# Two attention sums and one sum of activations, each at another place in VectorE's queue, in an attention and MLP block

## The chip, the cores and the metric

The kernel runs on one core of one Trainium2 chip. The metric is the time of one execution on the device in microseconds (us), inputs and outputs in the chip's memory. Engines go by these names: PE is TensorE (matmuls; PEld its weight loads), DVE is VectorE, ACT is ScalarE, POOL is GpSimd, and SP issues the DMA transfers. Each engine works through its own queue of instructions strictly in order; an instruction that waits for another engine holds up all that stand behind it in its queue.

## The reference

One block, on 2048 tokens of width 576, in float32:

```
xn  = layernorm(x)
q, k, v = xn @ wqkv                      # 32 heads of 18
att = softmax over 8 keys (this token and 7 before it, every second one) of q.k / sqrt(18)
out = x + (att @ v) @ wo + mish(xn @ w1 + b1) @ w2      # w1: 576 x 4608, w2: 4608 x 576
```

Tokens before the first are masked out of the softmax. All inputs and outputs are float32.

## The kernel before, in words

**Precision.** A float32 matrix is held as a high part in a rounded matmul format and a low part, the rest. A product is then three matmuls: high by high, high by low, low by high. Each operand made on the chip therefore takes two steps: ACT casts the high part (`u_high`, L820), and DVE or POOL subtracts it from the original to get the low part (`u_low`, L826).

**Tiling.** The tokens are done in two halves of 1024, each in blocks of 512. The 4608 hidden units are taken 256 at a time; one such step is called q. For each q, `m1_part` computes the hidden units of a half in six parts (numbered 0 to 5) out of blocked sums, in the manner of Strassen and Winograd, into three PSUM tiles h1, h2 and h3 (tag `h`, 4 buffers). ACT and DVE bring them to SBUF tiles (ACT copy at L714, DVE addition at L725, ACT Mish at L726). These activation tiles have the names `ra`, `rm`, `rt` with a number, and `ra_r`.

**The seven-product stage.** In the second half, the steps q = 0 to 7 are joined in pairs, e = 0 to 3, and the product with w2 of a pair is done as seven items (e, k), k = 0 to 6, of the products named P7, P4, P1, P5, P2, P6, P3 in that order. Each item is one call of `p_item`: 24 matmuls (L872) into four PSUM tiles `po` (tag `out`, 4 buffers), whose left operands are two tiles `u` (`u_e_k_0` and `u_e_k_1`, qq = 0 and 1) and whose right operand `pw` is fetched from memory. Each `po` is then added to an accumulator `accP...` by DVE (L878), or in the first pair, for three of the products, copied by ACT (L876). With four buffers, the first `po` of an item cannot begin before the first `po` of the item before has been read. Some left operands are sums of activations (`u_sum`, L814, on DVE or POOL), made in place in an activation tile.

**Attention alongside.** Attention needs no PE. It runs on POOL, DVE and ACT behind the matmuls, as a generator that goes on by one step at chosen places. A step multiplies on POOL, in two instructions (L539 for q by k, tiles `pr`; L577 for weights by v, tiles `pv`; the two share two buffers), and a DVE reduction sums the product (L544 into `L`, or L583 into `og`): these reductions are the attention sums. The sum of one step is kept back in `behind` and issued by `flush()` when the next step begins.

**What sets the order.** `plan` is a list of slots. Each slot has one part of PE's work (an `m1_part`, an item, a chunk of a product), and a list of background functions that `before(slot, fn)` puts there. For each slot the program issues, in this order: things left over for the beginning (`first`), the background functions, then what mish left pending in the slot before (`held`), then the slot's own work; and at the very end what lies in `tail`. Since each engine keeps the order in which its instructions were issued, this list is the schedule. `flush()` (L515 on) has three ways: normally the attention sum is issued at once, ahead of the slot's own additions; if the slot is in `behind_adds`, the sum goes to `tail`, behind everything of the slot; if it is in `behind_next`, it goes to the background list of the next slot.

The places of `u_sum`, `u_high` and `u_low` of an item come from a table of three numbers per (k, qq), `ds`: slots relative to that of the item. Slots are named by `at[...]`: `at["p", "x", e, k]` is that of the item (e, k), and `at["s", 1, q, i]` the i-th slot of step q in the second half.

Of the kernel before, what the change touches and what calls it, by code (L numbers as in the profile page):

```python
# [31 lines left out]
OC = 4  # L32
# [7 lines left out]
def block_kernel(ctx: ExitStack, tc: tile.TileContext, x, wq, wo, w1, b1, w2, mask, out):  # L40
# [469 lines left out]
    behind_adds, behind_next, now = set(), set(), [0]  # L510
# [296 lines left out]
    def u_sum(e, k, qq):  # L807
        name, q = LEFT[ORD[k]], 2 * e + qq
        eng = nc.gpsimd if (name, qq) in (("S1", 1), ("S4", 0)) else nc.vector
        x, y, op = dict(S3=("A11", "A21", ALU.subtract), S2=("A22", "S3", ALU.subtract), S1=("A11", "S2", ALU.add),  # L810
                        S4=("A12", "S2", ALU.subtract)).get(name, (None,) * 3)
        if x:
            t = rslotof(q, SLOT[name])
            eng.tensor_tensor(out=t, in0=u_src(q, x), in1=u_src(q, y), op=op)  # L814
            held_[q, SLOT[name]] = name
# [21 lines left out]
    def p_fetch(e, k):  # L837
        name = RIGHT[ORD[k]]
        t = pw[e, k] = sb.tile([P, 2, 2, HC], F32R, tag="w2", bufs=4, name=f"pw_{e}_{k}")
        nc.sync.dma_start(t.bitcast(F32), kept[name, e])  # L840
# [315 lines left out]
    at = {}  # L1156
# [7 lines left out]
    def before(i, fn):  # L1164
        plan[max(i, 0)][1].append(fn)
# [190 lines left out]
    def spot(hf, q, i):  # L1356
        return at["s", hf, q, i]
# [67 lines left out]
    for g, (e, k, s) in enumerate(items):  # L1425
        lead = items[g - 3][2] if g >= 3 else spot(1, 0, 5) + 2 * g
        before(lead + 1, lambda e=e, k=k: p_fetch(e, k))
        for qq in range(2):
            ds = {(0, 0): (-6, -5, -5), (0, 1): (-2, -1, -1), (1, 0): (0, -4, -2), (1, 1): (0, -2, -2), (2, 0): (0, -3, -2), (2, 1): (0, -3, -2), (3, 0): (-4, -3, -2), (3, 1): (-4, -2, -1), (4, 0): (0, -3, -3), (4, 1): (0, -3, -2), (5, 0): (-1, -3, -3), (5, 1): (0, -3, -2), (6, 0): (-4, -3, -1), (6, 1): (-4, -3, -2)}[k, qq]
            if (e, k, qq) == (OC - 1, 0, 0):  # L1430
                ds = (-5, -4, -4)
            if e == 0 and k in (3, 5):
                ds = (-3, -2, -1) if k == 3 else (1,) + ds[1:]
            for d, f in zip(ds[1:], (u_high, u_low)):
                before(s + d, lambda f=f, e=e, k=k, qq=qq: f(e, k, qq))
            s2 = items[7 * e + (0 if k == 5 else k)][2] + ds[0]
            before(s2, lambda e=e, k=k, qq=qq: u_sum(e, k, qq))
# [22 lines left out]
    for n in range(8):  # L1460
        c, k = divmod(n, 4)
# [30 lines left out]


    att = {}
    behind_adds.add(at["p", "x", OC - 1, 4])
    behind_next.add(at["m", 1, 10, 3])
    T = [0.0]
    for p_ in plan:
# [17 lines left out]
    k = marks[0] - 1  # L1516
    for n in range(steps - len(last_steps)):
        t = 6.111 * n
        k = next(k for k in range(k + 1, len(plan)) if T[k + 1] > t and ok[k])
# [21 lines left out]
    for n, name in enumerate(("T3", "T1", "T2", "T4", "B11", "B21", "B22", "R", "D")):  # L1541
        k = i + 10 + (2, 5, 10, 15, 20, 25, 30, 35, 40)[n]
# [77 lines left out]
```

## Time and profile before

| | us |
|---|---|
| median of 3 runs | 1109.92 |
| lowest and highest of them | 1109.09, 1110.12 |
| the profiled execution, own time | 1110.25 |
| its span, first to last instruction | 1108.5 |
| PE busy | 1100.6 |
| DVE busy | 851.2 |
| POOL busy | 789.4 |
| ACT busy | 499.1 |

The granted TensorE clock is at full speed over the whole span. The seven-product stage runs in the trace from about 625 to 827 us. Of the views used below: the chain of waits is the work that ended last, followed back from the end, with start, length and engine of each piece; the timeline lists the instructions of an engine with start (us), length (us), engine, line, what is written from what, the shape, and, in square brackets, how long the engine sat idle before it and for whom. An instruction's length overlaps a little with the start of the next; where the pace counts, differences of starts are taken.

### The profile page before, as it was taken

The numbers are of one execution on the slowest core, as the hardware profiler recorded it, in microseconds if no ns is written. First come the engines' busy times: TensorE is split into PE (matmuls) and PEld (weight loads), VectorE is DVE, ScalarE is ACT, GpSimd is POOL, SyncE is SP. The second block draws the span as 40 slices with busy tenths as digits, with TensorE's granted clock in tenths as the row PEclk, the third lists the DMA queues.
The fourth block names the chain that finished last, engine by engine and source line by source line (L and its number), as shares of the span: only waits on it lengthen the run. The fifth ranks groups of instructions, "written<-read, shape, count | busy, mean of one in ns | idle before, by whom it ended". The sixth has DMA issues, their size and how long they took to land.

```text
span 1108.5 us, 18208 instructions
## 1 busy us (share of the span) xinstructions
PE 1100.6 (99%) x6550; PEld 1014.4 (92%) x6550; DVE 851.2 (77%) x1367; ACT 499.1 (45%) x917; POOL 789.4 (71%) x639
## 2 busy tenths in 40 slices
PE   8999999999999999999999999999999999999998
PEld 7999899999999999999999888989899999999998
DVE  6368788888889888898656577777876677777786
ACT  5444655544545543545333354434433344343353
POOL 2479777776779688685789666667598976867542
PEclk9999999999999999999999999999999999999999
DMA  5899696868777768675598799656664657776674
GB/s 197 285 310 309 234 341 237 282 235 264 256 262 247 263 227 295 235 265 216 169 323 269 237 360 315 224 190 208 222 223 171 210 195 222 241 290 216 182 232 141
DMA packets 178271, 271.60 MB, mean 245 GB/s; under 512 B 53219, under 2 KB 120069, under 8 KB 178181
## 3 DMA queue, kind: packets, MB, share of 16 engines
q1 hardware_dynamic: 178180, 270.44, 71.8%
q8 instruction: 52, 0.85, 0.3%
q14 instruction: 39, 0.31, 0.1%
HBM read 160.39 MB, written 110.00 MB: 244 GB/s over the span
## 4 chain that ended last, share of the span: by engine, by line
PE 94%; DMA 2%; DVE 1%; ACT 1%; POOL 1%; issue 1%; SPq 0%; DVEq 0%; POOLq 0%
PE h L680 29%; PE po L780 21%; PE po L893 11%; PE pq L348 11%; PE po L872 7%; PE h L686 6%; PE o L1076 5%; PE z L446 4%; DMA acc<-in_x 1%; DMA accP<-in_x 1%; POOL act L732 0%; PE ta L75 0%; DVE rm L814 0%; DVE og L583 0%; ACT u L820 0%
## 5 line engine op out<-in xcount | busy, mean ns | idle before, releaser
L780 PEld LDWEIGHTS po<-w,act 128*128 128x128 f32 x1728 | 236.4, 188 | 6.0 <-POOL act L732 0.4
L780 PE MATMUL po<-w,act 128*128 128x288 f32 x1728 | 240.7, 295 | 0.2 <-POOL act L732 0.2
L539 POOL TENSOR_TENSOR pr<-q,kv 128x576 f32<-128x576 f32 x128 | 197.3, 1568 | 9.6 <-DMA q<-q_d 6.5
L732 POOL TENSOR_TENSOR act<-c,act 128x512 fp32r<-128x512 f32 x81 | 107.2, 1324 | 128.4 <-ACT act L731 127.8
L577 POOL TENSOR_TENSOR pv<-L,kv 128x576 f32<-128x576 f32 x128 | 178.1, 1484 | 24.8 <-DVE L L570 19.9
L784 DVE TENSOR_TENSOR acc<-po,acc 128x288 f32<-128x288 f32 x288 | 119.6, 450 | 30.0 <-PE po L780 28.8
L348 PE MATMUL pq<-wq,xt 128*128 128x432 f32 x672 | 136.4, 361 | 1.5 <-ACT xt L81 1.4
L893 PEld LDWEIGHTS po<-w,act 128*128 128x128 f32 x960 | 130.9, 188 | 2.9
L893 PE MATMUL po<-w,act 128*128 128x288 f32 x960 | 132.9, 294 | 0.0
L348 PEld LDWEIGHTS pq<-wq,xt 128*128 128x128 f32 x672 | 125.0, 188 | 8.4 <-ACT xt L81 2.4
L726 ACT ACTIVATE c<-c,b1c 128x512 f32<-128x512 f32 x81 | 58.7, 725 | 137.8 <-DVE c L725 137.6
L680 PE MATMUL h<-S,t 128*128 128x512 f32 x432 | 110.5, 391 | 0.0
L680 PE MATMUL h<-xt,t 128*128 128x512 f32 x432 | 110.5, 391 | 0.0
L583 DVE TENSOR_REDUCE og<-pv 128x144 f32<-128x1152 f32 x64 | 85.9, 1345 | 24.0 <-POOL pv L577 23.9
L680 PE MATMUL h<-xt,wa 128*128 128x512 f32 x432 | 104.1, 390 | 0.0
L714 ACT COPY c<-h 128x512 f32<-128x512 f32 x81 | 47.4, 586 | 124.2 <-PE h L686 73.1
L544 DVE TENSOR_REDUCE L<-pr 128x64 f32<-128x1152 f32 x64 | 85.8, 1342 | 19.7 <-POOL pr L539 19.6
L680 PEld LDWEIGHTS h<-xt,wa 128*128 128x128 f32 x432 | 80.9, 188 | 17.0
L872 PEld LDWEIGHTS po<-pw,u 128*128 128x128 f32 x672 | 92.0, 188 | 4.3 <-DVE accP L878 1.8
L872 PE MATMUL po<-pw,u 128*128 128x288 f32 x672 | 94.0, 295 | 1.1 <-DVE accP L878 0.9
L680 PEld LDWEIGHTS h<-xt,t 128*128 128x128 f32 x432 | 79.1, 188 | 14.7 <-DVE rt L725 0.2
L896 DVE TENSOR_TENSOR accP<-po,accP 128x288 f32<-128x288 f32 x160 | 69.0, 453 | 30.4 <-PE po L893 29.6
(228 smaller groups left out, 1853.2 us busy)
## 6 DMA issues: line engine op xcount, KB each, us to landing
kv<-kv_d SPq DMA_DIRECT2D x64, 396.0 KB, 4.9
kept_t<-t SPq DMA_DIRECT2D x36, 512.0 KB, 4.9
t<-kept_t SPq DMA_DIRECT2D x36, 512.0 KB, 6.3
rw<-in_w SPq DMA_DIRECT2D x36, 320.0 KB, 4.5
kept_wa<-wa SPq DMA_DIRECT2D x18, 640.0 KB, 5.0
kept_w<-w SPq DMA_DIRECT2D x20, 576.0 KB, 4.0
wa<-kept_wa SPq DMA_DIRECT2D x18, 640.0 KB, 5.3
w<-kept_w SPq DMA_DIRECT2D x20, 576.0 KB, 4.2
```

Of the source, the lines that this page charges most:

```text
L348: nc.tensor.matmul(pq[:, 0:432], XT[:, xi, tok], wt[wi][:, hl, 0:432], start=i == 0, stop=i == len(seq) - 1)
L539: nc.gpsimd.tensor_tensor(out=pr[:, x:x + hh], in0=q[:, j0 + x:j0 + x + hh, None, :].to_broadcast([P, hh, W, CU]), in1=win(kt, 0, CU, j0 + ...
L544: nc.vector.tensor_reduce(L[:, k, j0:j0 + hj].rearrange("p j w h -> p (j w h)"), pr.rearrange("p j w (h d) -> p (j w h) d", h=2), axis=AX, ...
L577: nc.gpsimd.tensor_tensor(out=pr[:, x:x + hj].rearrange("p j d w -> p j w d"), in0=L[:, k, x:x + hj, :, h:h + 1].to_broadcast([P, hj, W, DH]),
L583: nc.vector.tensor_reduce(og[:, c0:c0 + DH, :].rearrange("p d j -> p j d"), pr, axis=AX, op=ALU.add)
L680: nc.tensor.matmul(ph, wt[:, wl, wk * P:(wk + 1) * P], X[:, xs, :], start=first and i == 0, stop=last and i == len(seq) - 1, skip_group_ch ...
L732: nc.gpsimd.tensor_tensor(out=a[:, 1, :], in0=t, in1=a[:, 0, :].bitcast(F32), op=ALU.subtract)
L780: nc.tensor.matmul(po, acts[hf, q, b, j][:, al, tok], done["w2", hf, 2 * q + j][:, wl, c * HC:(c + 1) * HC], start=i == 0, stop=i == 5)
L784: nc.vector.tensor_tensor(out=t, in0=po, in1=t, op=ALU.add)
L872: nc.tensor.matmul(po, units[e, k, qq][:, al, tok], w[:, qq, wl, :], start=i == 0, stop=i == 5)
L893: nc.tensor.matmul(po, acts[hf, q, b, j][:, al, tok], done["w2", hf, 2 * q + j][:, wl, c * HC:(c + 1) * HC], start=i == 0, stop=i == 5)
L896: nc.vector.tensor_tensor(out=t, in0=po, in1=t, op=ALU.add)
```

## The change

Two slots join `behind_adds`: that of item (0, 4), and slot 1 of step 8, which is part 1 of `m1_part`. An attention sum that `flush()` would issue early in these slots is now issued last in them. And for e = 1, item k = 0, qq = 0 the three places in `ds` are one slot later each, as they were for the last pair already: the sum, its high and its low part.

```
-            if (e, k, qq) == (OC - 1, 0, 0):
+            if e in (1, OC - 1) and (k, qq) == (0, 0):
                 ds = (-5, -4, -4)
...
-    behind_adds.add(at["p", "x", OC - 1, 4])
+    behind_adds.update((at["p", "x", OC - 1, 4], at["p", "x", 0, 4], at["s", 1, 2 * OC, 1]))
```

(`OC` is 4; the general row of the table for (0, 0) is (-6, -5, -5).) No instruction is added or removed, and the orders of PE, ACT and SP are the same as before. DVE's order changes at two places and POOL's at one.

DVE's queue at the first place, around item (0, 4), before. `pr_1_1_0_0` is an attention product, `accP2` the accumulator of the item, `u_0_6_0` and `u_0_6_1` the left operands of item (0, 6), `rm0` the sum of activations for item (1, 0), `rt1` an addition that reads h3 of step 3:

```order
L544 TENSOR_REDUCE L_1_1_7745<-pr_1_1_0_0_7747 128x64
L878 TENSOR_TENSOR accP2_0_7472<-po_0_4_0_0_7812,accP2_0_7472 128x288
L878 TENSOR_TENSOR accP2_0_7472<-po_0_4_0_1_7820,accP2_0_7472 128x288
L878 TENSOR_TENSOR accP2_1_7473<-po_0_4_1_0_7828,accP2_1_7473 128x288
L878 TENSOR_TENSOR accP2_1_7473<-po_0_4_1_1_7836,accP2_1_7473 128x288
L826 TENSOR_TENSOR u_0_6_1_7846<-rm4_7263,u_0_6_1_7846 128x512
L814 TENSOR_TENSOR rm0_7259<-ra2_7257,rm0_7259 128x512
L725 TENSOR_TENSOR rt1_7265<-h3_1_3_7777,rt1_7265 128x512
L826 TENSOR_TENSOR u_0_6_0_7844<-ra3_7258,u_0_6_0_7844 128x512
```

The same stretch of DVE's queue in the changed kernel:

```order
L878 TENSOR_TENSOR accP2_0_7472<-po_0_4_0_0_7811,accP2_0_7472 128x288
L878 TENSOR_TENSOR accP2_0_7472<-po_0_4_0_1_7819,accP2_0_7472 128x288
L878 TENSOR_TENSOR accP2_1_7473<-po_0_4_1_0_7827,accP2_1_7473 128x288
L878 TENSOR_TENSOR accP2_1_7473<-po_0_4_1_1_7835,accP2_1_7473 128x288
L544 TENSOR_REDUCE L_1_1_7745<-pr_1_1_0_0_7747 128x64
L826 TENSOR_TENSOR u_0_6_1_7846<-rm4_7263,u_0_6_1_7846 128x512
L725 TENSOR_TENSOR rt1_7265<-h3_1_3_7777,rt1_7265 128x512
L826 TENSOR_TENSOR u_0_6_0_7844<-ra3_7258,u_0_6_0_7844 128x512
L814 TENSOR_TENSOR rm0_7259<-ra2_7257,rm0_7259 128x512
```

The attention sum has moved from ahead of the four additions to behind them, and the sum `rm0` from ahead of `rt1` and `u_0_6_0` to behind both.

POOL's queue at the same place, before (`u_1_0_0` is the low part of that same `rm0`):

```order
L814 TENSOR_TENSOR ra3_7258<-ra3_7258,rm2_7261 128x512
L539 TENSOR_TENSOR pr_1_1_0_1_7807<-q_1_2_7447,kv0_1_2_7445 128x576 x2
L826 TENSOR_TENSOR u_1_0_0_7900<-rm0_7259,u_1_0_0_7900 128x512
L539 TENSOR_TENSOR pr_1_1_1_0_7906<-q_1_3_7488,kv0_1_3_7486 128x576 x2
L539 TENSOR_TENSOR pr_1_1_1_1_7967<-q_1_3_7488,kv0_1_3_7486 128x576 x2
```

And POOL's queue there in the changed kernel:

```order
L814 TENSOR_TENSOR ra3_7258<-ra3_7258,rm2_7261 128x512
L539 TENSOR_TENSOR pr_1_1_0_1_7806<-q_1_2_7447,kv0_1_2_7445 128x576 x2
L539 TENSOR_TENSOR pr_1_1_1_0_7903<-q_1_3_7488,kv0_1_3_7486 128x576 x2
L826 TENSOR_TENSOR u_1_0_0_7914<-rm0_7259,u_1_0_0_7914 128x512
L539 TENSOR_TENSOR pr_1_1_1_1_7967<-q_1_3_7488,kv0_1_3_7486 128x576 x2
```

The low part `u_1_0_0` now stands behind the attention product `pr_1_1_1_0`, not ahead of it.

DVE's queue at the second place, the first slots of step 8, as the difference of the two kernels (`ra2` is an activation that ACT's Mish waits for, `og` an attention output, `accP7` the accumulator of item (3, 0)):

```order
 L826 TENSOR_TENSOR u_3_0_1_8929<-ra_r_7801,u_3_0_1_8929 128x512
 L814 TENSOR_TENSOR rm0_7259<-rt0_7264,rm0_7259 128x512
+L725 TENSOR_TENSOR ra2_7257<-h2_1_8_8916,ra2_7257 128x512
 L583 TENSOR_REDUCE og_1_2_8848<-pv_1_2_0_0_8849 128x8x18
-L725 TENSOR_TENSOR ra2_7257<-h2_1_8_8916,ra2_7257 128x512
 L814 TENSOR_TENSOR ra_r_7801<-rt1_7265,ra_r_7801 128x512
 L878 TENSOR_TENSOR accP7_0_7529<-po_3_0_0_0_8957,accP7_0_7529 128x288
```

The attention sum into `og` now comes behind the addition into `ra2`.

## The prediction, made before the changed kernel was run

> **What bounds the kernel now.** First the page of the profile: span, busy times, chain of waits.
>
> ```profile
> span 1108.5 us, 18208 instructions
> PE 1100.6 (99%) x6550; PEld 1014.4 (92%) x6550; DVE 851.2 (77%) x1367; ACT 499.1 (45%) x917; POOL 789.4 (71%) x639
> ```
>
> PE is busy for 1100.6 of 1108.5 us: it is the bound, and no change that leaves its matmuls as they are can win more than the 7.9 us between. No other engine is above 77%. So the question is only where PE waits, and whether the change touches those waits. The next view is PE's own timeline at the two places of the change, and, as a measure of the pace without a wait, the same kind of work in step 5.
>
> ```profile
> 705.47 3.33 PE L872 MATMUL po<-pw,u 128*128 128x288 f32 x24
> 708.64 1.53 PE L680 MATMUL h<-S,t 128*128 128x512 f32 x6
> 710.01 0.64 PE L686 MATMUL h<-xt,wc 128*128 128x512 f32 x2
> 710.48 3.33 PE L872 MATMUL po<-pw,u 128*128 128x288 f32 x24
> ```
>
> From start to start, an item takes 708.64 - 705.47 = 3.17 us, six L680 matmuls 1.37, and a pair of L686 0.47; one matmul of an item is 3.17 / 24 = 0.13. Now the first place:
>
> ```profile
> 684.77 0.61 PE L686 MATMUL h<-xt,wc 128*128 128x512 f32 x2
> 686.30 3.44 PE L872 MATMUL po<-pw,u 128*128 128x288 f32 x24 [0.92 <-DVE accP L878]
> 689.58 1.54 PE L680 MATMUL h<-xt,t 128*128 128x512 f32 x6
> ...
> 691.41 3.33 PE L872 MATMUL po<-pw,u 128*128 128x288 f32 x24
> ```
>
> Item (0, 5) would begin at 684.77 + 0.47 = 685.24 and begins at 686.30: 1.06 us late, and the bracket names DVE's additions into `accP`. It then takes 689.58 - 686.30 = 3.28, 0.11 above the pace, as the pipeline fills again. The wait costs 1.17 us. The second place:
>
> ```profile
> 795.61 3.77 PE L872 MATMUL po<-pw,u 128*128 128x288 f32 x24
> 799.22 1.53 PE L680 MATMUL h<-S,t 128*128 128x512 f32 x6
> 800.59 0.63 PE L686 MATMUL h<-xt,wc 128*128 128x512 f32 x2
> 801.24 3.44 PE L872 MATMUL po<-pw,u 128*128 128x288 f32 x24
> ```
>
> Item (3, 1) takes 799.22 - 795.61 = 3.61, 0.44 above the pace. Item (3, 2) starts 0.65 after the L686 pair where 0.47 is the pace, 0.18 late; its length of 3.44 is that of the late item above, so 0.11 more for refilling. Together 0.44 + 0.18 + 0.11 = 0.73 us. What ends last in each wait is read from the chain of waits (start, length, work):
>
> ```profile
> 682.84 1.78 DVE rm L814
> 684.62 1.26 DVE L L544
> 685.88 0.38 DVE accP L878
> ...
> 790.32 1.70 DVE rm L814
> 792.02 1.26 DVE og L583
> 793.28 0.61 DVE ra L725
> 793.91 0.55 ACT ra L726
> 794.54 0.61 ACT u L820
> 795.23 1.30 POOL u L826
> 796.57 2.81 PE po L872 x19
> ```
>
> At both places an attention sum of 1.26 us (L544, L583) lies in the chain that PE waits for. At the first it stands right ahead of the addition that frees the `po` buffer. At the second it stands ahead of the addition into `ra2`; ACT's queue waits there for that, with the cast of `u_3_1_1` behind it, then POOL takes its low part, and PE needs that for the sixth matmul of item (3, 1): 19 of 24 come after it.
>
> **Part one: the sum behind the additions of item (0, 4).** DVE and POOL around the place, now:
>
> ```profile
> 684.54 1.34 DVE L544 TENSOR_REDUCE L<-pr 128x64 f32<-128x1152 f32 x1
> 685.80 1.54 DVE L878 TENSOR_TENSOR accP<-po,accP 128x288 f32<-128x288 f32 x4
> 687.26 0.68 DVE L826 TENSOR_TENSOR u<-rm,u 128x512 fp32r<-128x512 f32 x1
> 687.86 0.68 DVE L814 TENSOR_TENSOR rm<-ra,rm 128x512 f32<-128x512 f32 x1
> 688.46 0.68 DVE L725 TENSOR_TENSOR rt<-h,rt 128x512 f32<-128x512 f32 x1
> 689.06 0.68 DVE L826 TENSOR_TENSOR u<-ra,u 128x512 fp32r<-128x512 f32 x1
> ```
>
> ```profile
> 682.33 1.74 POOL L814 TENSOR_TENSOR ra<-ra,rm 128x512 f32<-128x512 f32 x1
> 684.04 3.25 POOL L539 TENSOR_TENSOR pr<-q,kv 128x576 f32<-128x576 f32 x2
> 691.68 1.30 POOL L826 TENSOR_TENSOR u<-rm,u 128x512 fp32r<-128x512 f32 x1 [4.39 <-ACT u L820]
> ```
>
> The four additions take 687.26 - 685.80 = 1.46, the sum 1.26. With the two exchanged the additions begin at 684.54; the first ends by about 685.0 (a quarter of 1.54 after its start), before PE wants the buffer at 685.24, and the other three come 0.37 apart while PE asks for a new `po` each 3.17 / 4 = 0.79. The wait of 1.17 goes. The cover is thin, 0.2 us: were the sum before (`rm4`, 1.78 long) that much later, part of the wait would be back. That the `po` of item (0, 4) are ready is no condition: PE has left that item by 684.77 - 1.37 = 683.40. The displaced sum ends at 687.3. Who waits for it is POOL, whose next product wants the buffer that it reads; POOL is in the product before until 684.04 + 3.25 = 687.29, so nothing is lost there.
>
> **Part two: `rm0` one slot later.** DVE then goes on at 687.26 as today, with `u_0_6_1`, but `rt1` now at 687.86 and `u_0_6_0` at 688.46, each 0.60 earlier, and `rm0` last. This matters since the earlier PE wants h3, which `rt1` reads, at 685.24 + 3.17 = 688.41 instead of 689.58: with `rm0` still ahead, `rt1` would end at 689.14 and PE would wait 0.7. Now `rt1` ends at 688.54: 0.13 late, with refilling about 0.2. I take 0.2 as lost. `u_0_6_0` is needed for the third matmul of item (0, 6), at 688.61 + (691.41 - 689.58) + 0.26 = 690.70.
>
> POOL used to stand idle for 4.39 us, behind the low part `u_1_0_0`, waiting for ACT's cast. Now the product `pr_1_1_1_0` is ahead of it and fills that gap from about 687.9 to 691. That is work done earlier on POOL, worth nothing for PE by itself, but it runs beside DVE. What this costs is shown by the row of `rm4`: POOL's L814 lies from 682.33 to 684.07, DVE's subtraction that starts at 682.84 takes 1.78 and not 0.68, and ends at 684.62, 0.55 after POOL's. An operation of two SBUF operands on DVE that meets a busy POOL thus pays up to 1.10; the sum L544 beside `pr` shows 1.34 and no such rise. `u_0_6_0` at 688.46 meets the first half of the product (half of 3.25, so until about 689.5) and would end at about 690.1: 0.6 before PE wants it. `rm0` behind it may pay the full 1.10 and end near 692; its cast on ACT and low part on POOL come about a microsecond later than today's 691.68, while item (1, 0), for which they are, begins only at 691.41 + 3.17 + 4 x 1.37 + 2 x 0.47 = 701.0 today, 700.0 then. Cost nothing, cover some 6 us.
>
> The Trainium skill, "SBUF — State Buffer", section "Who interferes with whom", says that a VectorE instruction with two SBUF inputs and a GpSimd instruction that reads SBUF block each other wholly, whichever came first holding the port, and that a `tensor_reduce` on this chip never does. The rows of `rm4` and L544 above agree. By that rule `u_0_6_1` too would pay if POOL's product got in ahead of it; the sum would then be that of the second rival below.
>
> **Part three: the sum behind the addition into `ra2`.** `ra2` moves from 793.28 to 792.02, and so do ACT's Mish, the cast and POOL's low part, which POOL was idle for: it ends at 795.23 + 1.30 - 1.26 = 795.27, and PE needs it at 795.61 + 5 x 0.13 = 796.27. The 0.44 goes with 1.0 us to spare. (These are today's times; what the first place wins brings PE and these chains forward alike.) Next, item (3, 2):
>
> ```profile
> 796.48 2.53 POOL L826 TENSOR_TENSOR u<-ra,u 128x512 fp32r<-128x512 f32 x2
> ```
>
> ```profile
> 799.48 1.34 DVE L583 TENSOR_REDUCE og<-pv 128x144 f32<-128x1152 f32 x1
> 800.74 1.54 DVE L878 TENSOR_TENSOR accP<-po,accP 128x288 f32<-128x288 f32 x4
> ```
>
> The two low parts on POOL, DVE's S1 sum behind the first of them, the next attention sum and the additions all follow that low part and come up to 1.26 earlier: the first addition starts at 799.48 and ends by 799.9, PE wants its buffer at 798.78 + 1.37 + 0.47 = 800.62. So the 0.18 + 0.11 go too. The displaced sum ends at 793.8, where DVE stands today as well, so the additions of item (3, 0) are not later; `pv`, whose buffer it frees, comes after those low parts.
>
> **The sum.** 1.17 - 0.2 + 0.73 = 1.70 us less, by the profiled execution: 1110.25 - 1.70 = 1108.55 of its own time (its span is 1108.5; 1.75 lie around it). The median of the runs is 0.33 below the profiled one, 1109.92, so 1108.2. The ends: 1.17 + 0.73 = 1.90 if `rt1` is in time, and 0.56 by the second rival.
>
> **The rivals.**
>
> (1) Both waits go, the forecast: 1108.2. For it: all moved operations are in the chains that PE is shown to wait for, and after 686.30 PE goes on without a wait to the second place, and after 801.24 to the stage's end.
>
> (2) The port takes the first place back. If POOL's product begins before `u_0_6_1`, that pays 1.10, `rt1` ends at 689.64 and PE waits 1.23 for h3 with 0.11 to refill: first place 1.17 - 1.34 = -0.17, second +0.73, in all 0.56 less: 1110.25 - 0.56 is 1109.7 of the profiled time, 1109.4 beside the median. Against it: DVE reaches `u_0_6_1` at 687.26 straight behind the sum, for whose end POOL must first be told.
>
> (3) The gain is used up later: engines that kept pace with today's PE may not with one that is 1 us ahead, and PE waits at another place for as long. Margins of 0.2 to 1 us, as above, make it possible; that PE is followed by the other engines through its own results speaks against. With the whole 1.70 used up: 1109.9.
>
> (4) Slower: `ra_r`, the DVE addition behind `rm0` and the next attention sum, gets late. ACT's Mish of it, and behind that the Mish that reads h1 of step 3, stand in one queue; PE wants that h1 buffer for the second product of step 4. The addition's row today:
>
> ```profile
> 691.61 0.69 DVE L725 TENSOR_TENSOR ra_r<-h,ra_r 128x512 f32<-128x512 f32 x1 [0.61 <-PE h L686]
> ```
>
> By my count it moves from 691.61 to about 693.2 (`rm0` to 692, the sum 1.26) and ends at 693.9. PE wants the buffer at 691.41 + 3.17 + 2 x 1.37 + 0.47 = 697.8 today, about 696.8 then. Three ACT operations of 0.55 to 0.61 (the pieces in the chain above) lie between, so an end of the addition by 695.0 costs nothing; beyond it PE waits one for one, and from 696.7 on the 1.70 is eaten up. At 698.9 the kernel would be 2.2 us slower, 1112.1. That is 5 us above my count, four or five more payments of 1.10 to the port, and I see only one more operation that could pay, `u_0_6_1`.
>
> **How the numbers follow.** Chances: (1) 0.69, (2) 0.13, (3) 0.10, (4) 0.08. A difference of 0.2% (2.2 us) is about what a measurement of this kernel can tell from no change. The forecast, 1.7 us or 0.15%, lies just inside it, and medians of runs that spread over 1.03 us (1109.09 to 1110.12) can carry it half a microsecond to either side; of the 0.69 I put 0.34 beyond the bound and 0.35 within. With (2) and (3) within, and (4) slower: faster 0.34, same 0.58, slower 0.08. The range reaches from the full 1.90 with 1.1 us for the spread, 1106.9, up to rival (3) and its spread, 1110.3; (4) is left out. The forecast's own range is 1107.5 to 1108.9.
>
> **What would show it.** In the changed profile item (0, 5) starts about 0.5 us after the L686 pair ahead of it, with no bracket for `accP`; PE's next six matmuls wait at most 0.2 for `rt`; item (3, 1) lasts 3.33 and not 3.77, (3, 2) follows its pair after 0.47; POOL's idle 4.39 before `u_1_0_0` is mostly gone; PE's busy time stays near 1100.6 and the span is about 1106.8. I am wrong if a new PE wait for DVE (h3, `u_0_6_0`) or for ACT (step 4) of a microsecond stands between 688 and 702, or if PE stops anew between 700 and 827.

## The result, and the profile after

| us | before | changed |
|---|---|---|
| median of 21 runs each, on one chip | 1110.01 | 1108.83 |
| lowest and highest | 1109.09, 1112.48 | 1107.92, 1109.51 |
| the profiled execution, own time | 1110.25 | 1109.51 |
| its span | 1108.5 | 1107.7 |

The ratio of the times is 0.9986, with a 95% interval of 0.998 to 0.9992: 1.55 us less (0.0014 x 1110.01), between 0.9 and 2.2. The medians stand 1.18 apart. A second set on another chip (below) gave 1108.85 against 1110.63, ratio 0.9984 (0.9975 to 0.9992). The change makes the kernel faster by about a microsecond and a half, inside the 0.2% named as the bound of what counts as a difference; both intervals lie below 1 all the same, so less than 0.2% could be told from no change here. In a few executions of several kernels here the mean granted clock was 0.997 or 0.998 and the time some microseconds longer; this widens an interval, and hardly moves a median.

One thing to know before the rows are read: the profiled execution of the changed kernel was the slowest of its 21 runs. What is behind that, the experiments show further down.

The page of the changed kernel, its span and busy times:

```profile
span 1107.7 us, 18208 instructions
PE 1100.8 (99%) x6550; PEld 1015.3 (92%) x6550; DVE 850.6 (77%) x1367; ACT 499.1 (45%) x917; POOL 791.1 (71%) x639
```

PE's timeline in the changed kernel at the second place:

```profile
795.51 3.33 PE L872 MATMUL po<-pw,u 128*128 128x288 f32 x24
798.68 1.53 PE L680 MATMUL h<-S,t 128*128 128x512 f32 x6
800.05 0.64 PE L686 MATMUL h<-xt,wc 128*128 128x512 f32 x2
800.53 3.38 PE L872 MATMUL po<-pw,u 128*128 128x288 f32 x24
```

Item (3, 1) takes 798.68 - 795.51 = 3.17 where it took 3.61, and item (3, 2) starts 0.48 after its pair where it started 0.65 after. Both waits are gone. Now the first place, PE's timeline:

```profile
684.32 0.61 PE L686 MATMUL h<-xt,wc 128*128 128x512 f32 x2
685.74 3.47 PE L872 MATMUL po<-pw,u 128*128 128x288 f32 x24 [0.81 <-DVE accP L878]
689.29 1.66 PE L680 MATMUL h<-xt,t 128*128 128x512 f32 x6
690.79 0.62 PE L686 MATMUL h<-xt,wa 128*128 128x512 f32 x2
691.24 0.96 PE L872 MATMUL po<-pw,u 128*128 128x288 f32 x6
```

The wait for the additions is still there: item (0, 5) starts 1.42 after its pair, 0.95 late by the pace of 0.47. It then takes 3.55, 0.38 above the pace, because it ends in a wait for `rt1`, and the six L680 after it take 0.13 more than 1.37. In all 1.46 us, more than the 1.17 of before. Yet DVE's order is the one that was wanted, as its timeline in the changed kernel shows, with POOL's below it:

```profile
683.55 1.77 DVE L814 TENSOR_TENSOR rm<-rm,rm 128x512 f32<-128x512 f32 x1
685.24 1.54 DVE L878 TENSOR_TENSOR accP<-po,accP 128x288 f32<-128x288 f32 x4
686.70 1.34 DVE L544 TENSOR_REDUCE L<-pr 128x64 f32<-128x1152 f32 x1
687.96 0.68 DVE L826 TENSOR_TENSOR u<-rm,u 128x512 fp32r<-128x512 f32 x1
688.56 0.68 DVE L725 TENSOR_TENSOR rt<-h,rt 128x512 f32<-128x512 f32 x1
689.16 1.32 DVE L826 TENSOR_TENSOR u<-ra,u 128x512 fp32r<-128x512 f32 x1
690.41 1.92 DVE L814 TENSOR_TENSOR rm<-ra,rm 128x512 f32<-128x512 f32 x1
...
693.51 0.68 DVE L725 TENSOR_TENSOR ra_r<-h,ra_r 128x512 f32<-128x512 f32 x1
```

```profile
684.73 7.04 POOL L539 TENSOR_TENSOR pr<-q,kv 128x576 f32<-128x576 f32 x4
693.05 1.29 POOL L826 TENSOR_TENSOR u<-rm,u 128x512 fp32r<-128x512 f32 x1 [1.28 <-ACT u L820]
```

The additions stand straight behind `rm4`, the sum behind them. But `rm4` starts at 683.55, where it started at 682.84 before: 0.71 later, while PE's pair was 0.45 earlier (684.32 against 684.77). What made DVE late stands far ahead of the place, in the chain of waits of the same execution (start, length, work):

```profile
656.58 8.82 DMA t<-kept_t
...
665.41 8.29 DMA accP<-in_x
...
673.84 1.43 POOL accP L858
...
675.67 0.45 DVE accP L878
...
683.55 1.77 DVE rm L814
685.32 1.46 DVE accP L878 x4
...
689.29 1.66 PE h L680 x6
```

A part of x, with which an accumulator starts, lands at 673.70. POOL then subtracts the part of P5 from that of P3 (L858, `x_diff`, two instructions); DVE's additions of item (0, 3), which go into the accumulator of P5, wait for the second of them. What DVE does from there to item (0, 4)'s additions stands behind in its queue, with one detour over ACT: a Mish and two casts, from 680.48 to 682.24, for which DVE sits idle 1.82 us in both kernels. The row of that subtraction in POOL's timeline, first of the kernel before, then of the changed one:

```profile
673.12 1.43 POOL L858 TENSOR_TENSOR accP<-accP,accP 128x576 f32<-128x576 f32 x1 [0.88 <-DMA accP<-in_x]
```

```profile
673.83 1.43 POOL L858 TENSOR_TENSOR accP<-accP,accP 128x576 f32<-128x576 f32 x1 [1.50 <-DMA accP<-in_x]
```

It is 0.71 later in the changed kernel, exactly as much as `rm4`. The wait for the transfer was there before, too; the prediction followed the chain back to `rm4` and stopped there.

### The profile page after: what moved, and what is told of

Its sections match the earlier page's. It is cut to its first block, busy times and chain, and to the rows that moved or that the text cites. A ratio compares the mean times of both kernels' runs of the same rounds, so it can differ in the third digit from the quotient of the medians.

```text
span 1107.7 us, 18208 instructions
## 1 busy us (share of the span) xinstructions
PE 1100.8 (99%) x6550; PEld 1015.3 (92%) x6550; DVE 850.6 (77%) x1367; ACT 499.1 (45%) x917; POOL 791.1 (71%) x639
## 4 chain that ended last, share of the span: by engine, by line
PE 94%; DMA 2%; DVE 2%; ACT 1%; POOL 1%; issue 0%; SPq 0%; DVEq 0%; POOLq 0%
PE h L680 29%; PE po L780 21%; PE po L893 11%; PE pq L348 11%; PE po L872 6%; PE h L686 6%; PE o L1076 5%; PE z L446 4%; DMA t<-kept_t 1%; DMA accP<-in_x 1%; POOL act L732 0%; PE ta L75 0%; DMA acc<-in_x 0%; DVE st L112 0%; DVE u L826 0%
## 5 line engine op out<-in xcount | busy, mean ns | idle before, releaser
L680 PE MATMUL h<-xt,t 128*128 128x512 f32 x432 | 110.7, 391 | 0.1
L680 PE MATMUL h<-S,t 128*128 128x512 f32 x432 | 110.5, 391 | 0.0
L680 PE MATMUL h<-xt,wa 128*128 128x512 f32 x432 | 104.1, 390 | 0.0
L680 PEld LDWEIGHTS h<-xt,wa 128*128 128x128 f32 x432 | 80.9, 188 | 17.0
L680 PEld LDWEIGHTS h<-xt,t 128*128 128x128 f32 x432 | 79.1, 188 | 15.1 <-DVE rt L725 0.5
```

The lines of the kernel that those rows point to most:

```text
L680: nc.tensor.matmul(ph, wt[:, wl, wk * P:(wk + 1) * P], X[:, xs, :], start=first and i == 0, stop=last and i == len(seq) - 1, skip_group_ch ...
```

## The experiments

Two theories stood to be told apart. By the prediction, the first place is a matter of PE's pace and of the order on DVE and POOL near it, and each part of the change is worth the same in every execution. By the other, the first place starts with the landing of that part of x: from the second L858 to PE's six L680 behind item (0, 5) the way has a fixed length, which the change shortens, and a late landing comes through to the end one for one. In the texts that were recorded ahead of the runs, theory A is that an exchange is worth what it takes out of the chain that PE waits for, wherever that chain begins; the second theory here is theory A with the landing as the beginning. Theory B there is that the landing ends the first place whatever the order behind it, so that the whole gain comes from the second place. The table has for each profiled execution the start of the second L858 (T0), of those six L680 (T1), of item (0, 6) (T2), and the span; the rows "again" are second runs of the same programs, told of further down.

| kernel | T0 | T1 - T0 | T2 | T2 - T0 | span | span - T2 |
|---|---|---|---|---|---|---|
| before | 673.12 | 16.46 | 691.41 | 18.29 | 1108.5 | 417.1 |
| second place only | 673.17 | 16.47 | 691.47 | 18.30 | 1107.9 | 416.4 |
| first place, sum only | 673.17 | 16.08 | 691.19 | 18.02 | 1108.3 | 417.1 |
| first place, shift only | 673.74 | 16.73 | 692.42 | 18.68 | 1109.6 | 417.2 |
| first place, both | 673.43 | 15.48 | 690.86 | 17.43 | 1107.9 | 417.0 |
| changed | 673.83 | 15.46 | 691.24 | 17.41 | 1107.7 | 416.5 |
| changed again | 673.14 | 15.48 | 690.57 | 17.43 | 1107.0 | 416.4 |
| changed, x part later | 675.88 | 15.46 | 693.29 | 17.41 | 1109.8 | 416.5 |
| changed, x parts earlier | none | | 689.77 | | 1106.3 | 416.5 |
| changed, x parts earlier, again | none | | 689.60 | | 1106.1 | 416.5 |
| before, x parts earlier | none | | 690.11 | | 1107.2 | 417.1 |

("None" is where the second L858 no longer waits for a transfer.) The last column is the second place by itself: 416.4 to 416.5 with its edit, 417.0 to 417.2 without. T2 - T0 is the first place by itself: 17.41 to 17.43 with both of its edits, whether T0 is 673.14 or 675.88. What is left to differ between profiles of kernels with the same edits is T0. Theory B is out by these columns: with both edits the way behind the landing is 0.86 shorter (17.43 in place of 18.29).

**The second place alone.**

```
-    behind_adds.add(at["p", "x", OC - 1, 4])
+    behind_adds.update((at["p", "x", OC - 1, 4], at["s", 1, 2 * OC, 1]))
```

> Only slot 1 of step 8 joins the set; item (0, 4) and the table row stay as before. Theory A (each exchange is worth what it takes out of the chain that PE waits for, wherever that chain begins): 0.7 us less than before, ratio 0.9994, item (3, 1) at 3.33 and (3, 2) 0.47 behind its pair, and the wait for accP ahead of item (0, 5) as in the kernel before, about 1.2. Theory B (the first place ends with the landing of a part of x, so that the order behind it hardly counts, and the whole measured gain of 1.2 us is from the second place): 1.2 us less, ratio 0.9989.

Measured: 1109.67 against 1110.58 for the kernel before on the same chip (11 or 12 executions of each changed program here and below), ratio 0.9995 (0.9986 to 1.0003). The interval alone would not tell it from nothing; the profile does, with a span 0.6 shorter while T0 and T2 are the same to 0.06. At the first place PE's wait is untouched:

```profile
686.36 3.44 PE L872 MATMUL po<-pw,u 128*128 128x288 f32 x24 [1.36 <-DVE accP L878]
```

The second place is worth 0.6 to 0.7 by itself, with the first place as it was.

**The first place alone, with both of its edits.**

```
-            if (e, k, qq) == (OC - 1, 0, 0):
+            if e in (1, OC - 1) and (k, qq) == (0, 0):
...
-    behind_adds.add(at["p", "x", OC - 1, 4])
+    behind_adds.update((at["p", "x", OC - 1, 4], at["p", "x", 0, 4]))
```

> Item (0, 4) joins the set and the row for e = 1 is one slot later; step 8 stays as before. Theory A: 0.9 us less than before, ratio 0.9992, and counted from the end of the second subtraction of x parts (POOL L858) to the six matmuls behind item (0, 5) it is about 0.9 shorter than before, whatever the time of the landing. Theory B: no difference, ratio 1.0000.

Measured: 1109.30 against 1110.58, ratio 0.9989 (0.9981 to 0.9998); the span is 0.6 shorter, with a T0 0.31 later than that of before. PE's timeline still has part of the wait:

```profile
685.35 3.44 PE L872 MATMUL po<-pw,u 128*128 128x288 f32 x24 [0.61 <-DVE accP L878]
```

From T0 to item (0, 6) it takes 17.43 and not 18.29: the two edits take 0.86 out of that way. What PE then sees of it depends on where T0 falls.

**The sum alone, without the shift of `rm0`.**

```
-    behind_adds.add(at["p", "x", OC - 1, 4])
+    behind_adds.update((at["p", "x", OC - 1, 4], at["p", "x", 0, 4]))
```

> Item (0, 4) joins the set; the row for e = 1 stays, so that the sum rm0 is still ahead of rt1 on DVE. Theory A: the additions free the buffer 1.26 earlier, but rt1 comes no earlier than before, so PE waits for h3 instead: of the 0.9 some 0.6 is lost, 0.3 us less than before, ratio 0.9997; PE waits about 0.8 for rt ahead of the six matmuls behind item (0, 5). If the shift does nothing for PE: 0.9 less, as with both edits.

Measured: 1110.38 against 1110.58, ratio 1.0005 (0.9996 to 1.0014): nothing. PE's timeline:

```profile
685.41 3.33 PE L872 MATMUL po<-pw,u 128*128 128x288 f32 x24
689.25 1.65 PE L680 MATMUL h<-xt,t 128*128 128x512 f32 x6 [0.51 <-DVE rt L725]
```

The wait for the additions is gone, item (0, 5) starts at the pace (0.45 after its pair at 684.96), and PE waits at the next thing: the item and the wait take 3.84, 0.67 above the pace. The prediction had put that at 0.7 for this very case. Of the 0.86, the sum alone keeps 0.27.

**The shift alone.**

```
-            if (e, k, qq) == (OC - 1, 0, 0):
+            if e in (1, OC - 1) and (k, qq) == (0, 0):
```

> Only the row for e = 1 is one slot later; both attention sums stay as before. Theory A: the wait for accP ahead of item (0, 5) stays at about 1.2, rt1 is then 0.6 early for nothing, no difference, ratio 1.0000; POOL's idle time before the low part of rm0 is mostly gone all the same. If work of POOL done earlier is itself worth something: up to 0.5 us less.

Measured: 1110.67 against 1110.58, ratio 1.0007 (0.9995 to 1.0018). The way from T0 to item (0, 6) is 0.39 longer than before. POOL, DVE and PE in this kernel, a timeline each:

```profile
684.65 6.45 POOL L539 TENSOR_TENSOR pr<-q,kv 128x576 f32<-128x576 f32 x4
```

```profile
685.15 1.34 DVE L544 TENSOR_REDUCE L<-pr 128x64 f32<-128x1152 f32 x1
...
687.87 1.94 DVE L826 TENSOR_TENSOR u<-rm,u 128x512 fp32r<-128x512 f32 x1
689.74 0.68 DVE L725 TENSOR_TENSOR rt<-h,rt 128x512 f32<-128x512 f32 x1
```

```profile
686.92 3.44 PE L872 MATMUL po<-pw,u 128*128 128x288 f32 x24 [1.55 <-DVE accP L878]
690.47 1.66 PE L680 MATMUL h<-xt,t 128*128 128x512 f32 x6
```

This is the mechanism of the second rival, seen at work. Here the attention sum stands ahead of the additions and ends at 686.5, so POOL's second product has its buffer and follows the first without a gap: its first instruction, the third of the four in the row, starts at 687.83. `u_0_6_1`, 0.04 behind it at 687.87, takes 1.94 instead of 0.68. In the changed kernel the sum ends only at 688.04 and that instruction of POOL starts at 688.12, 0.16 behind `u_0_6_1` (687.96), so DVE gets in first: 0.68, and the four instructions of POOL take 7.04 together instead of 6.45. The Trainium skill, "SBUF — State Buffer", section "Who interferes with whom", says that it is the order of issue that decides who blocks; the two rows of the same instruction, 0.68 and 1.94, agree. For this run that was not expected: `rt1` was to come 0.6 early, and counted from T0 it starts 0.66 later than before (16.00 in place of 15.34). So each of the two edits is worth little or less than nothing alone (0.27, -0.39), and 0.86 together: the shift frees `rt1`, and the sum behind the additions keeps POOL out until `u_0_6_1` has begun.

**The changed kernel with the parts of x fetched earlier.** The test of the landing by moving it: of the transfers of x parts (`x_send`, L854), P5 and P3 are issued one slot earlier. On SP they then stand ahead of the right operand of item (0, 4) and of two transfers for later work.

```
-        before(i - (1 if name == "P3" else 2), lambda name=name, pr=pr: x_send(name, pr))
+        before(i - (2 if name == "P3" else 3 if name == "P5" else 2), lambda name=name, pr=pr: x_send(name, pr))
```

> The changed kernel, with the parts of x for P5 and P3 asked for one slot earlier, so that the last of them is ahead of two other transfers in SP's queue. Theory A with the landing as the start of the chain: the second subtraction of x parts (POOL L858) no longer waits for a transfer, DVE's queue at item (0, 4) comes about 1 us earlier, the wait for accP ahead of item (0, 5) falls from 0.8 to under 0.3, and the kernel is 0.8 to 1.3 us below the changed one, ratio to before 0.9976. If the landing does not matter: as the changed kernel, 0.9986.

Measured: 1108.20 against 1110.37, ratio 0.9989 (0.9977 to 1.0002); ten of the twelve executions lie between 1108.04 and 1108.65, and the other two, at 1114.86 and 1113.92, make the interval so wide that it does not exclude 1. POOL's timeline, then PE's:

```profile
670.80 2.85 POOL L858 TENSOR_TENSOR accP<-accP,accP 128x576 f32<-128x576 f32 x2
```

```profile
684.78 3.33 PE L872 MATMUL po<-pw,u 128*128 128x288 f32 x24
687.95 1.53 PE L680 MATMUL h<-xt,t 128*128 128x512 f32 x6
```

Both subtractions now run one behind the other with no wait, DVE is ahead of PE, and at the first place PE has no wait at all: 0.45 from the pair at 684.33 to the item, 3.17 for the item, and also none for `rt1`.

**The changed kernel with one part of x later.** The other way: the two transfers of P3's part are issued one slot later.

```
-        before(i - (1 if name == "P3" else 2), lambda name=name, pr=pr: x_send(name, pr))
+        before(i - (0 if name == "P3" else 2), lambda name=name, pr=pr: x_send(name, pr))
```

> The changed kernel, with the parts of x for P3 asked for one slot later, behind two or three other transfers. Theory A with the landing as the start of the chain: the last of them lands 2 to 3 us later and PE waits that much longer ahead of item (0, 5) or for h3: 2 to 3 us above the changed kernel, ratio to before 1.0005 to 1.0015. If the landing does not matter: as the changed kernel, 0.9986.

Measured: 1111.56 against 1110.37, ratio 1.0011 (1.0002 to 1.0019). The subtraction on POOL and item (0, 5) on PE:

```profile
675.88 1.43 POOL L858 TENSOR_TENSOR accP<-accP,accP 128x576 f32<-128x576 f32 x1 [1.59 <-DMA accP<-in_x]
```

```profile
687.78 3.44 PE L872 MATMUL po<-pw,u 128*128 128x288 f32 x24 [0.86 <-DVE accP L878]
```

T0 is 2.05 later than in the changed kernel, T1 and T2 2.05, the span 2.1. The way between keeps its length to 0.02. Even with the change in it, the kernel is then a little slower than before.

**The kernel before with the parts of x fetched earlier.** The edit of `x_send` that fetches the parts early, made in the kernel before.

> The kernel before, with the parts of x for P5 and P3 asked for one slot earlier, no other edit. Theory A with the landing as the start of the chain: the chain begins about 1 us earlier, so that the sum ahead of the additions nearly hides; of the 1.2 waited ahead of item (0, 5) 0.9 goes, ratio 0.9992. The first place's edit is then worth little on top of it: between this kernel and the changed one with the same early parts there lie the 0.7 of the second place and about 0.3. If the landing does not matter: 1.0000.

Measured: 1109.12 against 1110.37, ratio 0.9986 (0.9977 to 0.9994). PE at the first place:

```profile
684.38 0.61 PE L686 MATMUL h<-xt,wc 128*128 128x512 f32 x2
684.99 3.47 PE L872 MATMUL po<-pw,u 128*128 128x288 f32 x24
688.30 1.53 PE L680 MATMUL h<-xt,t 128*128 128x512 f32 x6
```

Without the change in it, an earlier landing alone takes most of the first wait away: item (0, 5) is 0.14 late and 0.14 long, 0.28 in place of 1.17, about as expected. Against the changed kernel with early parts, T2 is 0.34 later, 0.05 of which lies ahead of the L686 pair (684.38 against 684.33), and the kernel is 0.92 slower (1109.12 against 1108.20 on one chip), of which the second place has some 0.6. So the change is worth about 0.3 at the first place where the landing is early, and 0.86 where it is late.

**The changed kernel once more, beside the version with early parts.** The first run had profiled the slowest of its executions, so both kernels ran again on one chip.

> The changed kernel itself, beside the next one and the kernel before on one chip. Chain from the landing: 1.0 to 1.6 us below before, ratio 0.9988; from the second subtraction of x parts (POOL L858) to the six matmuls behind item (0, 5) again 15.5 us; executions spread over about 1 us, since the landing does.

> The changed kernel with the parts of x for P5 and P3 asked for one slot earlier, as in the run of that edit before, beside the changed kernel on one chip. Chain from the landing: 0.6 to 1.0 us below the changed kernel, 2.0 to 2.3 below before, ratio 0.9980, and undisturbed executions within 0.4 us of each other, since PE waits for no landing at that place any more. If the earlier run was an accident of its chip: as the changed kernel.

Measured, against 1110.63 for the kernel before: the changed kernel 1108.85 (1108.29 to 1109.62), ratio 0.9984 (0.9975 to 0.9992); with early parts 1108.18 (1107.78 to 1109.98), ratio 0.998 (0.9971 to 0.9989). In the profiled execution of the first of them the landing came as early as in the kernel before; POOL and PE:

```profile
673.14 1.43 POOL L858 TENSOR_TENSOR accP<-accP,accP 128x576 f32<-128x576 f32 x1 [0.96 <-DMA accP<-in_x]
```

```profile
684.70 0.62 PE L686 MATMUL h<-xt,wc 128*128 128x512 f32 x2
685.15 3.39 PE L872 MATMUL po<-pw,u 128*128 128x288 f32 x24
688.62 1.66 PE L680 MATMUL h<-xt,t 128*128 128x512 f32 x6
690.11 0.62 PE L686 MATMUL h<-xt,wa 128*128 128x512 f32 x2
```

The two additions on DVE, `rt1` and `ra_r`, that are spoken of below:

```profile
687.88 0.68 DVE L725 TENSOR_TENSOR rt<-h,rt 128x512 f32<-128x512 f32 x1
...
692.82 0.68 DVE L725 TENSOR_TENSOR ra_r<-h,ra_r 128x512 f32<-128x512 f32 x1
```

Here the profile is the one that was forecast: item (0, 5) 0.45 after its pair, with no bracket, and then a short wait for `rt1` alone (3.47 for the item, 1.49 for the six). Against the first profile of the same program, T0 is 0.69 earlier, T2 0.67, the span 0.7, the execution's own time 0.66 (1108.85 against 1109.51). The changed kernel lies 1.78 below the one before by medians, somewhat more than the 1.0 to 1.6 expected. The version with early parts beats both: 0.67 below the changed one by medians and 2.45 below the one before, though single executions of the first two overlap. With no wait for the landing, the first place follows PE: in the two profiles with early parts item (0, 6) starts 5.44 behind the L686 pair, at 684.33 and 684.16, and the spans differ by about as much as these starts (1106.3 and 1106.1). The expectation that the undisturbed executions would lie within 0.4 of each other failed: ten of the eleven lie within 1.0.

## Why the prediction was right, and which terms were off

The time was forecast at 1108.2, with 1.70 us less than before and the larger part of the chance within 0.2%. Measured were 1108.83, inside the range, and 1.55 less by the ratio (1.78 in the second set). The range, 1106.9 to 1110.3, says little, since it also holds the time of the kernel before (1110.01); the forecast's own, 1107.5 to 1108.9, holds the measured median by 0.07. By its steps:

- **PE is the bound and only its waits can be won.** Right. Its span less its busy time was 7.9 before and is 6.9 in the profile after; the span is 1107.7 and in the second profile 1107.0, where about 1106.8 was named.
- **Part three, 0.73.** Right. Between the starts of item (3, 0) and of the L680 behind item (3, 2) 13.44 us became 12.77, 0.67 less; the second place's edit alone shortens the span by 0.6 at the same T2.
- **Part one, "The wait of 1.17 goes".** Right in the order of the work, and in one of the two profiles right as it stands. The step that failed is the cover: "The cover is thin, 0.2 us: were the sum before (`rm4`, 1.78 long) that much later, part of the wait would be back." `rm4` was later by 0.71 in the profiled execution, the wait was back with 0.95 (PE was also 0.45 earlier at the pair), and what moved `rm4` was a landing that the prediction did not look for. With the landing at 673.14, as before, the wait is gone.
- **Part two, `rt1` "0.13 late, with refilling about 0.2".** The mechanism was right, the term too small: with the landing as before, `rt1` ends at 688.56 against 688.54 forecast, but PE, which was through its pair 0.07 earlier and starts 0.06 behind the end of `rt1`, loses 0.30 before the six L680 and 0.12 in them, 0.42 in place of 0.2. The 0.97 forecast for the first place (1.17 - 0.2) is 0.84 by T2 at equal T0, and 0.86 to 0.88 in the way from T0. That `rm0` ahead of `rt1` would cost 0.7 was measured: 0.67.
- **`u_0_6_0` and `rm0` behind it pay up to 1.10 to POOL.** `u_0_6_0` takes 1.32, `rm0` 1.92 where the row used had 1.78; `ra_r`, counted to start at about 693.2, starts at 693.51 with the late landing and at 692.82 with the landing as before, and ends well ahead of the 695.0 named. The low part `u_1_0_0` comes at 693.05 and nobody waits for it: the idle time ahead of it on POOL fell from 4.39 to 1.28.
- **Rival two, the port.** Not in the changed kernel, where the argument against it (POOL must first be told of the sum's end) held, by 0.16 us; and seen with the shift alone: 1.26 us for `u_0_6_1`. The condition was named rightly; that the shift without the exchange would meet it was not said.
- **Rival three, the gain used up later.** Not so: span - T2 is 416.4 to 417.2 in every kernel, and the difference within it is that of the second place.
- **Rival four, slower by `ra_r`.** No PE wait for ACT follows. A slower kernel came from elsewhere, the landing 2 us later; the prediction had no rival on that side for a transfer.

So both terms came near, each a little too large: the way from T0 became 0.86 shorter in place of 0.97, the second place gave 0.6 to 0.7 in place of 0.73. Where the cover held, as in the second profile, it was by the luck of a landing no later than in the kernel before. What the prediction did not see is that 0.7 us of landing, by which two profiled executions of one program differed, weigh as much as the gain at the first place: the profiled pair shows only 1110.25 - 1109.51 = 0.74 less, which by the columns of the table is -0.88 at the first place, -0.6 at the second and +0.71 of landing, -0.77 in all. That the landing makes most of the difference between executions of one program is shown for these two; that it makes the spread of all of them is suggested by the narrower one of early parts (ten of twelve within 0.6 us, ten of eleven within 1.0 in the second set, against 1.3 and 1.6 for all executions of the changed kernel), and not shown.

Left open is why that part of x was issued when it was. In the chain of waits the landing of a 512 KB transfer `t` stands right ahead of the issue, in both profiles of the changed kernel. The view of SP's waits points the same way: ahead of that issue SP waits for `t` by 0.9 us in the first profile of the changed kernel, 0.9 with both edits of the first place, 0.6 with the shift alone and 0.4 with the second place alone, and not at all in the kernel before, with the sum alone and in the second profile of the changed kernel; the three latest T0 (673.83, 673.74, 673.43) are those with 0.6 or more. No run moved `t` to test this, and why it took 8.82 us once and 7.59 the other time was not tried either.

## What to carry to other kernels

When a wait is to be removed, follow its chain back past the instruction that you move, to the first piece with a wait of its own; if that is a transfer, ask how much its landing differs from execution to execution before a cover of 0.2 us is called a cover. Two edits around one wait may be worth something only together, since the second takes what the first uncovers. And before an order on the engines is tuned, see whether an earlier issue of one transfer does the same: here one changed line took 1.25 us from the kernel before by itself (medians on one chip), at the same ratio to it as the change, 0.9986.

## What was not expected of the hardware

The stretches of the trace from 660 to 672 us, in the kernel before and in the changed one (length, busy time of PE, PEld, DVE, ACT and POOL, granted clock, DMA share, GB/s):

```profile
660.00:672.00 12.00, 12.00 (x81) 11.32 (x80) 7.19 (x9) 5.10 (x11) 10.71 (x9) 1.00 1.05 390
```

```profile
660.00:672.00 12.00, 12.00 (x81) 11.32 (x80) 5.90 (x9) 5.29 (x11) 10.35 (x9) 1.00 1.05 388
```

The DMA engines are busy throughout. A part of x (288 KB) took about the same time from issue to landing in all three profiles, 8.20 us in the kernel before, 8.29 in the changed one and 8.25 in its second profile, as the last one's chain of waits shows:

```profile
657.15 7.59 DMA t<-kept_t
...
664.75 8.25 DMA accP<-in_x
```

It was the issue, at 665.41 in the slowest execution and 664.75 in the other, that was 0.66 late, not the transfer (0.04). In such a stretch it counts when SP gets to a transfer: one slot earlier in its queue took POOL's wait of 0.9 to 1.5 us away altogether, and one slot later delayed everything behind it by 2.05.
